# Loading wq straight into the tile that the matmuls read, in two halves and in its own column order

## The chip, the cores and the metric

The kernel runs on one core of a Trainium2 chip. The time is the device time of one execution in microseconds (us). Three runs of the kernel before gave 731.84, 732.01 and 732.11 us; the median, 732.01 us, is the number to compare with.

## The reference: what is computed

Two attention blocks, A and B, with the same shapes and their own inputs; their outputs are put side by side (16 x 64 x 1280). One block:

```python
B, Sq, D, H, Sk, Dh = 16, 64, 640, 32, 512, 128
q = (x @ wq).reshape(B, Sq, H, Dh).transpose(0, 2, 1, 3)
scores = einsum("bhqd,bhkd->bhqk", q, k_cache) * Dh ** -0.5
p = softmax(scores)
o = einsum("bhqk,bhkd->bhqd", p, v_cache)
out = o.transpose(0, 2, 1, 3).reshape(B, Sq, H * Dh) @ wo
```

All inputs are bf16. k_cache and v_cache are 67.1 MB each per block, so 268.4 MB of the 295 MB that are moved; wq and wo are 5.2 MB each per block. Each byte of the caches is read once.

## The kernel before, in words

**Packs.** The work is cut into 128 packs. A pack is four heads of two batch entries: 1.05 MB of K, 1.05 MB of V. Four packs (`NJ = 4`, index j) share one pair of batch entries and so one transposed x. Eight such groups make a phase of 32 packs, in which the same 16 heads' columns of wq (2.6 MB) and rows of wo (2.6 MB) are used. There are four phases: two halves of the heads for each of the two blocks.

**Operations of pack n**, by the names in the plan: `LDK`, `LDV` (loads into rings of 6 and 4 packs), `KT` (VectorE transposes K in 32x32 blocks of 32-bit words, L702), `QP` (20 matmuls x times wq into PSUM, L688), `QE` (ScalarE copies q to SBUF, L694), `S` (scores, L712), `EX` (ScalarE exp with row sums, L741), `RC` and `NM` (reciprocal on VectorE, normalisation on GpSimd, L762), `TR` (p is transposed on TensorE, L774), `TE` (VectorE copies it to SBUF, L854), `PV` (L867), `OE` (L875), `OP` (times wo, L887), and after each fourth pack `OS` and, in the phases that finish a block, the store `ST`. Once per group x is loaded and transposed: `LDX`, `XT` (L662), `XE`, `XS` and `XC` (GpSimd copies it to `xT_ring`, L677).

**Order.** No order is found at run time. `build_plan` gives every operation a due time in packs (`n + AT[...]`), sorts each engine's operations by it, and derives semaphore waits from the tiles that they read and write; a wait that follows from another one is left out. Each engine then works through its list in order. All loads but the first x are issued by SyncE (SP), in one list sorted by a priority that is also counted in packs: `LDK(n)` has n - 4.6, `LDV(n)` n - 2.1, `LDWO` of phase 0 n - 1.9 and of later phases n - 1.4. SP issues a load only when its buffer is free; what stands behind it waits too. `LDV(n)` waits for `TR(n-3)` in this way. Packs -1 and -2 are run on zeros, so that TensorE's list can be a loop of four packs from the first pack on.

**wq before.** `LDWQ` loads the 2.6 MB of a phase as five transfers (one for each 128 rows of D, 4096 bytes in a row) into a staging tile `ws_sb`, laid out like wq itself. In phase 0 all five stand at the head of SP's list, ahead of K. Those of phase 1 are issued at priority 1.85, those of phases 2 and 3 spread over the phase before. Eight operations `WP` per phase (GpSimd, L656, 128 x 1280 elements each, two for each j) copy the staging tile to `wqp_sb`; within each head they put the column 64 j' + 2 r + t at the place 4 r + 2 j' + t. `QP` reads its weights with a step of four elements, so that one weight load holds the columns whose partner words one 32-bit transpose of K brings to the same row. `KT` reads the K row of a token as 64 words in order (two blocks of 32) and writes runs of two words.

**Zeroing at the start.** On VectorE, in this order: `VZ` (two slots of the V ring, L594), `BZ` (four PSUM banks, L598), `WZ` (half of wo, L602). The zeroing of `pT_sb` for pack -2 (`TE(-2)`, L852) stands at its due time, -0.57 and -0.53, which is after `KT(0)` at -0.67. GpSimd zeroes `pn_ring` (`NM(-1)`, L760).

Of the kernel before, what the change touches and what calls it, by code (L numbers as in the profile page):

```python
# [20 lines left out]
class Cfg:  # L21
    NK = 6
# [18 lines left out]
              OPZ=(1.65, 1.7), OSH=(1.75, 1.8), STH=(1.85, 1.9), FL1=1.3, FLM=1.68, FLC=1.82, WP0=(-1.6, -1.59, -0.7, -0.69, 0.25, 0.26, 1.25, 1.26),  # L41
              WP1=(-3.5, -2.55, -2.45, -1.5, -0.5, 0.5, 0.6, 1.5))


class Op:
# [41 lines left out]
def build_plan(dims, cfg, general):  # L87
# [18 lines left out]
    def add_output(n):  # L106
        g, j = n // NJ, n % NJ
        final = n >= 0 and dims["FINAL"](g // NBP)
        apart = 0 <= n < cfg.KSPLIT or n >= N - cfg.NARROW
        for b in range(0 if apart else 1, 2):  # L110
            tv = n + AT["PV"]
            op = add("sp", "LDV", (n, b), tv - 0.3, [],
                     [("v" if n >= 0 else "absent", n % cfg.NV, i) for i in ((b,) if apart else (0, 1))])
            loads.append((n - cfg.NV + AT["PV"] + 0.2 if n >= 0 else -99.0, 3, op))
        if n == N - 1:
            for a in range(2):
                add("pe", "TRH", a, n + AT["TRH"][a], [("pn", n % cfg.NPN, i) for i in (2 * a, 2 * a + 1)] + [("ident",)],
                    [("SB", 2), ("SB", 3)] if a == 0 else [("SB", 0), ("SB", 1)])
# [12 lines left out]
        if n > -2:  # L131
            add("pe", "TR", n, n + AT["TR"], [("pn", n % cfg.NPN, i) for i in range(4)] + [("ident",)],
                [("B", 4), ("B", 5)])
        for b in range(2):
            add("dve", "TE", (n, b), n + AT["TE"][b], [], [("B", 4 + b), ("pT", b, 0), ("pT", b, 1)])
        add("pe", "PV", n, n + AT["PV"], [("pT", b, a) for b in range(2) for a in range(2)] + [("v", n % cfg.NV, 0), ("v", n % cfg.NV, 1)],
            [("B", 4), ("B", 5), ("B", 6), ("B", 7)])
        add("act", "OE", (n, 0), n + AT["OE"][0], [], [("B", 4), ("B", 5), ("oT", 0)])
        if n == N - 2:
            add("act", "OEH", (n, 1), n + AT["OE"][1], [], [("B", 6), ("B", 7), ("oT", 1)])  # L140
            for s in range(2):
                add("pe", "OPH", (n, s), n + 1 + AT["OPY"][s], [("oT", 0), ("oT", 1), ("wo", j)], [("B", 6 + s)])
            return
        add("act", "OE", (n, 1), n + AT["OE"][1], [], [("B", 6), ("B", 7), ("oT", 1)])
        add("act", "ZO", n, n + AT["ZO"], [("zeros",)], [("B", 6), ("B", 7)])
        add("pe", "OP", n, n + AT["OP"], [("oT", 0), ("oT", 1), ("wo", j)], [("B", 6), ("B", 7)])
        if j == NJ - 1:
            bp = g % NBP
            add("dve", "OS", g, n + AT["OS"], [("acc", bp)], [("B", 6), ("B", 7)]
                + ([("out_sb", 0), ("out_sb", 1)] if final else [("acc", bp)]))  # L150
            if final:
                loads.append((n + AT["ST"], 5, add("sp", "ST", g, n + AT["ST"], [("out_sb", s) for s in range(2)], [("out_dram", g)])))
# [17 lines left out]
                add("act", "LDX", g, -21.0, [], [("xn", g % cfg.NXN)])  # L170
        add("pool", "XC", g, n0 + AT["XC"], [("xe", 0), ("xe", 1)] if first else [("xs", g % NBP)], [("xT", g % cfg.NX)])
    for ph in range(NPH):
        twp = [ph * PH + t for t in AT["WP1" if ph else "WP0"]]
        for kt in range(dims["KT"]):
            ready = (twp[-1] - PH if ph > 1 else AT["WP0"][-1]) + 0.5
            op = add("sp", "LDWQ", (ph, kt), twp[0] - 0.5 if ph else -20.0, [], [("ws", kt, j) for j in range(NJ)])
            loads.append((ready + 2.0 + 0.14 * PH * kt if ph > 1 else AT["PV"] + 0.15 if ph else -50.0, 1, op))
        for j in range(NJ):
            w = ph * NJ + j
            n0 = ph * PH + j  # L180
            for i in range(2):
                add("pool", "WP", (w, i), twp[2 * j + i], [("ws", kt, j) for kt in range(dims["KT"])], [("wqp", j, i)])
            if ph:
                loads.append((n0 - NJ + AT["LDWO"], 4, add("sp", "LDWO", w, n0 + AT["OP"] - 0.8 * NJ, [], [("wo", j)])))
            else:
                loads.append((n0 - 1.9, 4, add("sp", "LDWO", w, n0 + AT["OP"] - 0.8 * NJ, [], [("wo", j)])))
    if not general:
        add("pool", "PZ", 0, -9.95, [], [("zeros",)])
    add("dve", "VZ", 0, -9.9, [], [("v", i % cfg.NV, b) for i in (-2, -1) for b in range(2)])
    add("dve", "BZ", 0, -9.8, [], [("B", 4), ("B", 5), ("B", 6), ("B", 7)])  # L190
    add("dve", "WZ", 0, -9.7, [], [("wo", NJ - 2), ("wo", NJ - 1)])
    add("pool", "NM", -1, -1 + AT["NM"][3], [], [("pn", -1 % cfg.NPN, i) for i in range(4)])
    for n in range(-2, N):
        add_output(n)
        if n < 0:
            continue
        g, j = n // NJ, n % NJ
        add("pe", "QP", n, n + AT["QP"], [("xT", g % cfg.NX), ("wqp", j, 0), ("wqp", j, 1)], [("SB", 1)])
# [54 lines left out]
    for op in ops:  # L253
# [27 lines left out]
    def stand_in(d, op):  # L281
# [223 lines left out]
def mha_kernel(nc, blocks, out, cfg=None):  # L505
# [26 lines left out]
    with contextlib.ExitStack() as es:  # L532
# [2 lines left out]
        def sb(name, shape, dt):  # L535
            return es.enter_context(nc.sbuf_tensor(name, shape, dt))

        wqp_sb = sb("wqp_sb", [128, NJ, KT, 512], BF16)
        wo_sb = sb("wo_sb", [128, HPH, D], BF16)
        ws_sb = sb("ws_sb", [128, KT, NJ, 512], BF16)  # L540
# [70 lines left out]
        def em_LDWQ(e, op):  # L611
            ph, i = op.idx
            c = ph % NSUB * HPH * DH
            src = blocks[ph // NSUB][3].rearrange("(kt p) n -> p kt n", p=128)
            ins = e.dma_start(ws_sb[:, i].rearrange("p j c -> p (j c)"), src[:, i, c:c + NJ * 512])  # L615
            return ins, ins

        def em_LDWO(e, op):
# [33 lines left out]
        def em_WP(e, op):  # L652
            j, jj = op.idx[0] % NJ, op.idx[1]
            src = ws_sb[:, :, j].rearrange("p k (i j r) -> p k i j r", i=4, j=2)
            dst = wqp_sb[:, j].rearrange("p k (i r j two) -> p k i j r two", i=4, j=2, two=2)
            ins = e.tensor_copy(dst[:, :, :, jj], src[:, :, :, jj].rearrange("p k i (r two) -> p k i r two", two=2))  # L656
            return ins, ins

        def em_XT(e, op):
            first = last = None  # L660
            for kt in range(KT):
# [18 lines left out]
        def em_QP(e, op):  # L680
# [1 line left out]
            j = n % NJ  # L682
            xs = (n // NJ) % NX
            first = last = None
            w = wqp_sb[:, j].rearrange("p k (c f) -> p k f c", f=4)
            for f in range(4):
                for kt in range(KT):
                    last = e.matmul(ps[:, 1, f * 128:(f + 1) * 128], w[:, kt, f, :], xT_ring[:, xs, kt, :],  # L688
# [9 lines left out]
        def em_KT(e, op):  # L698
            n = op.idx
            dst = kt_ring[:, n % NKT].rearrange("p t j b k two -> p (t j) b (k two)").bitcast(F32)  # L700
            src = kn_ring[:, n % NK].rearrange("p a c -> p (a c)").bitcast(F32).rearrange("p (c h b l) -> p c h b l", h=8, b=2, l=2)
            ins = e.transpose(dst.rearrange("p c b (h l) -> p c h b l", h=8, l=2), src)  # L702
            return ins, ins

        def em_S(e, op):
# [224 lines left out]
        emitters = {k[3:]: f for k, f in locals().items() if k.startswith("em_")}  # L930

        ahead = {}

        def units(key):
            return 16 if key[0].startswith("d_") else 1

        def emit(e, op, p, taken):
            sem = sems[p]
            waits = [(s, v - taken.get(s, 0)) for s, v in op.waits]
            attach = None  # L940
            if waits and not op.dma and op.kind != "FL1":
                attach = waits.pop()
            for s, v in waits:
                e.wait_ge(sem[s], v * units(s))
            kind = "EXG" if p and op.kind == "EX" else op.kind
            first, last = emitters[kind](e, op)
            if last is None:
                e.sem_inc(sem[op.sem], units(op.sem))
                return
# [121 lines left out]
```

## Time and profile before

| | |
|---|---|
| median of three runs | 732.01 us |
| the profiled execution: time, span | 732.12 us, 730.4 us |
| TensorE (PE) busy, granted clock | 674.1 us, 92%; 0.99 |
| VectorE (DVE), ScalarE (ACT), GpSimd (POOL) busy | 514.5, 533.3, 417.9 us |
| bytes moved by DMA | 295.02 MB, mean 404 GB/s |

Rows of the timeline and of the chain give start and duration in us. Rows of a group give line, engine, operation, tiles and shape, the count, then total us and mean ns of one, then the idle time before them with what ended it. A row of stretches gives, for a stretch A:B, its length, the busy time of PE, PEld (weight loads), DVE, ACT and POOL with their instruction counts, the granted clock of TensorE, the busy share of the 16 DMA engines and the GB/s moved. Issue rows of the DMA view end with the KB of each transfer and the median us from issue to landing. "issue" in the chain or behind a row is time in which the engine waited for nothing that the profile shows.

### The profile page before, as it was taken

To read this page: it belongs to the slowest core of one execution; us is meant where nothing else is said; L and a number is where in the kernel's file an instruction comes from. 1 tells how busy PE (TensorE), PEld (TensorE's weight loads), DVE (VectorE), ACT (ScalarE), POOL (GpSimd) and SP (SyncE) were. 2 spreads that over 40 slices of the span, in tenths; PEclk is the share of its full clock that TensorE was granted. 3 is DMA by queue.
4 is the path that set the end of the run, shared out by engine and by line. 5 is a ranking of instruction groups with operands and counts; after the bars stand their busy time and mean duration, and the time that the engine had idled before them with its cause. 6 is when DMAs were issued, how large, how long until landed. Compare 5 with 4: busy or idle time off the path is not lost.

```text
span 730.4 us, 61195 instructions
## 1 busy us (share of the span) xinstructions
PE 674.1 (92%) x28502; PEld 530.3 (73%) x28502; DVE 514.5 (70%) x691; ACT 533.3 (73%) x1574; POOL 417.9 (57%) x596
## 2 busy tenths in 40 slices
PE   1679999999999999999997899999999799999998
PEld 1458778787777777777775677787777577787775
DVE  5447777777777766767765667677777567878775
ACT  1447878778787777777875677777778677878775
POOL 4436565666875455554884555465587446555552
PEclk9889999999999999999999999999999999999999
DMA  8999999999999999999999999999999999999993
GB/s 337 401 404 414 414 415 413 415 414 415 415 400 409 419 414 416 416 416 417 416 411 402 415 414 413 414 415 415 414 416 407 403 415 418 417 418 417 416 415 122
DMA packets 72336, 295.02 MB, mean 404 GB/s; under 512 B 7664, under 2 KB 20080, under 8 KB 55920
## 3 DMA queue, kind: packets, MB, share of 16 engines
q1 hardware_dynamic: 72160, 294.52, 100.0%
q8 instruction: 10, 0.16, 0.1%
q10 hardware_dynamic: 144, 0.16, 0.1%
q14 instruction: 22, 0.18, 0.1%
HBM read 292.03 MB, written 2.62 MB: 403 GB/s over the span
## 4 chain that ended last, share of the span: by engine, by line
PE 53%; DMA 32%; SPq 6%; DVE 3%; issue 3%; POOL 2%; ACT 1%; DVEq 0%; POOLq 0%
DMA xn_ring<-in_B_x_dram 14%; PE ps L867 12%; PE ps L887 11%; PE ps L688 11%; PE ps L712 10%; DMA kn_ring<-in_A_k_cache_dram 9%; PE ps L774 7%; DMA kn_ring<-in_B_k_cache_dram 5%; DMA wo_sb<-in_B_wo_dram 4%; SPq L631 4%; DVE kt_ring L702 2%; POOL pn_ring L762 2%; SPq L641 1%; DVE pT_sb L854 1%; SPq L615 1%
## 5 line engine op out<-in xcount | busy, mean ns | idle before, releaser
L762 POOL TENSOR_SCALAR pn_ring<-pn_ring,recip 128x512 bf16<-128x512 bf16 x508 | 343.4, 695 | 246.1 <-DVE recip L754 221.0
L702 DVE STREAM_TRANSPOSE kt_ring<-kn_ring 128x2048 f32<-128x2048 f32 x128 | 295.3, 2307 | 120.3 <-DMA kn_ring<-in_B_k_cache_dram 80.3
L741 ACT ACTIVATE pn_ring<-ps 128x512 bf16<-128x512 f32 x512 | 296.4, 592 | 5.7 <-PE ps L712 5.7
L854 DVE COPY pT_sb<-ps 128x1024 bf16<-128x1024 bf16 x256 | 168.4, 671 | 60.2 <-PE ps L774 60.2
L688 PE MATMUL ps<-xT_ring,wqp_sb 128*128 128x128 bf16 x2560 | 165.9, 220 | 11.6 <-POOL xT_ring L677 11.6
L867 PE MATMUL ps<-pT_sb,v_ring 32*128 32x64 bf16 x16448 | 162.2, 192 | 10.6 <-DVE pT_sb L854 4.6
L688 PEld LDWEIGHTS ps<-xT_ring,wqp_sb 128*128 128x128 bf16 x2560 | 157.5, 114 | 17.8 <-issue 11.8
L867 PEld LDWEIGHTS ps<-pT_sb,v_ring 32*128 32x128 bf16 x16448 | 147.0, 91 | 24.8 <-issue 12.5
L887 PE MATMUL ps<-wo_sb,oT_sb 128*128 128x320 bf16 x1024 | 163.5, 303 | 0.0
L875 ACT ACTIVATE oT_sb<-ps 128x256 bf16<-128x256 f32 x257 | 84.7, 381 | 95.1 <-PE ps L867 95.1
L712 PE MATMUL ps<-kt_ring,qs_ring 32*64 32x512 bf16 x4096 | 138.4, 380 | 4.8 <-issue 4.8
L694 ACT ACTIVATE qs_ring<-ps 128x512 bf16<-128x512 f32 x128 | 76.4, 597 | 76.5 <-PE ps L688 74.5
L774 PEld LDWEIGHTS ps<-ident,pn_ring 64*128 64x128 bf16 x4096 | 68.3, 95 | 77.0 <-ACT oT_sb L875 46.0
L887 PEld LDWEIGHTS ps<-wo_sb,oT_sb 128*128 128x128 bf16 x1024 | 90.4, 98 | 36.7
L741 ACT ACTIVATION_READ_ACCUMULATOR pn_ring<-ps 128x1 f32 x512 | 105.3, 206 | 0.0
L774 PE MATMUL ps<-ident,pn_ring 64*128 64x64 bf16 x4096 | 82.9, 191 | 22.8 <-POOL pn_ring L762 18.6
L712 PEld LDWEIGHTS ps<-kt_ring,qs_ring 32*64 32x64 bf16 x4096 | 53.4, 103 | 32.9 <-issue 5.5
L754 DVE RECIPROCAL recip<-rowsum 128x2 f32<-128x2 f32 x256 | 40.6, 158 | 27.6 <-ACT pn_ring L741 24.6
L879 ACT ACTIVATE ps<-zeros 128x256 f32<-128x256 bf16 x128 | 49.5, 387 | 4.1
L656 POOL COPY wqp_sb<-ws_sb 128x1280 bf16<-128x1280 bf16 x32 | 39.6, 1256 | 9.9 <-DMA ws_sb<-in_A_wq_dram 6.8
L668 ACT ACTIVATE xe_sb<-ps 128x640 bf16<-128x640 bf16 x32 | 22.9, 716 | 8.7 <-PE ps L662 8.6
L677 POOL COPY xT_ring<-xe_sb 128x640 bf16<-128x640 bf16 x16 | 11.5, 717 | 21.0 <-PE ps L774 21.0
(42 smaller groups left out, 103.5 us busy)
## 6 DMA issues: line engine op xcount, KB each, us to landing
kn_ring<-in_B_k_cache_dram SPq DMA_DIRECT2D x128, 512.0 KB, 16.1
v_ring<-in_B_v_cache_dram SPq DMA_DIRECT2D x62, 1024.0 KB, 16.5
kn_ring<-in_A_k_cache_dram SPq DMA_DIRECT2D x112, 512.0 KB, 11.4
v_ring<-in_A_v_cache_dram SPq DMA_DIRECT2D x56, 1024.0 KB, 14.8
kn_ring<-in_A_k_cache_dram SPq DMA_DIRECT2D x32, 256.0 KB, 8.6
v_ring<-in_A_v_cache_dram SPq DMA_DIRECT2D x16, 512.0 KB, 8.9
ws_sb<-in_A_wq_dram SPq DMA_DIRECT2D x10, 512.0 KB, 9.3
wo_sb<-in_A_wo_dram SPq DMA_DIRECT2D x8, 640.0 KB, 13.3
```

The source lines that it names most:

```text
L688: last = e.matmul(ps[:, 1, f * 128:(f + 1) * 128], w[:, kt, f, :], xT_ring[:, xs, kt, :], start=(kt == 0), stop=(kt == KT - 1))
L694: ins = e.activation(qs_ring[:, op.idx % NQ].rearrange("p f b q -> p (f b q)"), ps[:, 1, :], ACTF.Copy, scale=scale)
L702: ins = e.transpose(dst.rearrange("p c b (h l) -> p c h b l", h=8, l=2), src)
L712: last = e.matmul(ps[64 * b:64 * b + 64, i, :], qs_ring[rows, n % NQ, f, b, :], kt_ring[rows, n % NKT, :, f // 2, b, :, f % 2], start=(f = ...
L741: ins = e.activation(dst, src, ACTF.Exp, scale=1.0, accum_out=sum_of(h))
L762: ins = e.tensor_scalar(pn_view(h), pn_view(h), recip[:, h:h + 1], 1.0, ALU.mult, ALU.mult)
L774: last = e.transpose(pt_bank(b)[:, 64 * c:64 * c + 64], pn[rows, c, :], ident[rows, rows], tile_position=(64 * b, 0))
L854: ins = e.tensor_copy(pT_sb[:, b].rearrange("p t q -> p (t q)"), pt_bank(b))
L867: last = e.matmul(ps[:, 4 + i, 64 * b:64 * b + 64], v_ring[rows, n % NV, b, c, :], pT_sb[rows, b, c, :], start=(t == 0 and i < 2), stop=(t ...
L875: ins = e.activation(oT_sb[:, 2 * a:2 * a + 2, :], o_ps[:, 2 * a:2 * a + 2, :], ACTF.Copy)
L879: ins = e.activation(z_ps, zeros[:, :].unsqueeze(2).broadcast_to([128, 2, 128]), ACTF.Copy)
L887: last = e.matmul(out_ps[:, s, :], oT_sb[:, i, :], wo_sb[:, 4 * j + i, s * NH0:(s + 1) * NH0], start=(j == 0 and i == 0), stop=(j == NJ - ...
```

## The change

- The staging tile `ws_sb` and the copies `WP` are gone. `LDWQ` writes `wqp_sb`, which now has wq's own column order, in two transfers per phase: columns of j = 0, 1 and columns of j = 2, 3, each 1.31 MB in pieces of 2048 bytes.
- In phase 0 the first half stands ahead of K (priority -50), the second half behind K of pack 0 (-4.0 against -4.6). In later phases the halves have priority -4.4 and -2.4, counted from the phase's first pack, and wait until TensorE has done the last `QP` of the phase before that reads the columns. For this a mark `QS` lets the first matmul of the operation after every second `QP` raise a semaphore.
- Who waits for wq: for packs 0 and 1 TensorE itself, with a wait `GO` ahead of `QP(0)`; for the first half of later phases `XC` on GpSimd; for second halves `NM(., 3)` of the pack two before the first `QP` that needs it, also on GpSimd.
- `QP` reads its weights at the same step of four elements as before. The permutation goes into `KT`: it reads the K words with a step of two (first the even, then the odd words of a token) and writes as before.
- `WZ` goes from VectorE to GpSimd, behind `XC(0)`. `TE(-2)` goes ahead of `KT(0)`.

```diff
-              OPZ=..., WP0=(-1.6, -1.59, -0.7, -0.69, 0.25, 0.26, 1.25, 1.26),
-              WP1=(-3.5, -2.55, -2.45, -1.5, -0.5, 0.5, 0.6, 1.5))
+              WQ=(-3.2, -4.4))
...
-            add("dve", "TE", (n, b), n + AT["TE"][b], ...)
+            add("dve", "TE", (n, b), n + AT["TE"][b] if n > -2 else AT["KT"] - 0.01 + 0.002 * b, ...)
...
-            op = add("sp", "LDWQ", (ph, kt), twp[0] - 0.5 if ph else -20.0, [], [("ws", kt, j) for j in range(NJ)])
-            loads.append((ready + 2.0 + 0.14 * PH * kt if ph > 1 else AT["PV"] + 0.15 if ph else -50.0, 1, op))
+        for i in range(2):
+            op = add("sp", "LDWQ", (ph, i), ph * PH + 2 * i + AT["WQ"][0] if ph else -20.0, [],
+                     [("wqp", j) for j in (2 * i, 2 * i + 1)])
+            loads.append((ph * PH + 2 * i + AT["WQ"][1] if ph else (-50.0, -4.0)[i], 1, op))
...
-                add("pool", "WP", (w, i), twp[2 * j + i], [("ws", kt, j) for kt in range(dims["KT"])], [("wqp", j, i)])
+    add("pe", "GO", 0, AT["QP"] - 0.001)
-    add("dve", "WZ", 0, -9.7, [], [("wo", NJ - 2), ("wo", NJ - 1)])
+    add("pool", "WZ", 0, AT["XC"] + 0.001, [], [("wo", NJ - 2), ("wo", NJ - 1)])
...
+        if j % 2:
+            add("pe", "QS", n, n + AT["QP"] + 0.001)
...
-        if op.kind == "QP" and op.idx > 0:
-            op.deps = [d for d in op.deps if d.kind != "WP"]
+        if op.kind == "QP":
+            n, j = op.idx, op.idx % NJ
+            at[("GO", 0) if n < 2 else ("XC", n // NJ) if j < 2 else ("NM", 4 * (n - j) + 3)].deps += [d for d in op.deps if d.kind == "LDWQ"]
+            op.deps = [d for d in op.deps if d.kind != "LDWQ"]
...
+        if d.kind == "QP" and op.eng == "sp":
+            return at[("QS", d.idx | 1)]
...
-            ins = e.dma_start(ws_sb[:, i].rearrange("p j c -> p (j c)"), src[:, i, c:c + NJ * 512])
+            ins = e.dma_start(wqp_sb[:, :, 1024 * i:1024 * i + 1024], src[:, :, c + 1024 * i:c + 1024 * i + 1024])
...
-            src = kn_ring[:, n % NK].rearrange("p a c -> p (a c)").bitcast(F32).rearrange("p (c h b l) -> p c h b l", h=8, b=2, l=2)
-            ins = e.transpose(dst.rearrange("p c b (h l) -> p c h b l", h=8, l=2), src)
+            src = kn_ring[:, n % NK].rearrange("p a c -> p (a c)").bitcast(F32)
+            src = src.rearrange("p (t h b l j) -> p t j h b l", h=8, b=2, l=2, j=2)
+            ins = e.transpose(dst.rearrange("p (t j) b (h l) -> p t j h b l", j=2, h=8, l=2), src)
...
+            if op.kind == "QS":
+                marks.append(sem[op.sem])
+                return
...
+            if op.eng == "pe" and marks:
+                first.then_inc(marks.pop(), 1)
```

More of the change, by code (lines that the diff above doesn't have):

```diff
@@ L134, in add_output @@
         for b in range(2):
-            add("dve", "TE", (n, b), n + AT["TE"][b], [], [("B", 4 + b), ("pT", b, 0), ("pT", b, 1)])
+            add("dve", "TE", (n, b), n + AT["TE"][b] if n > -2 else AT["KT"] - 0.01 + 0.002 * b, [], [("B", 4 + b), ("pT", b, 0), ("pT", b, 1)])
         add("pe", "PV", n, n + AT["PV"], [("pT", b, a) for b in range(2) for a in range(2)] + [("v", n % cfg.NV, 0), ("v", n % cfg.NV, 1)],
@@ L180, in build_plan @@
             n0 = ph * PH + j
-            for i in range(2):
-                add("pool", "WP", (w, i), twp[2 * j + i], [("ws", kt, j) for kt in range(dims["KT"])], [("wqp", j, i)])
             if ph:
@@ L197, in build_plan @@
         g, j = n // NJ, n % NJ
-        add("pe", "QP", n, n + AT["QP"], [("xT", g % cfg.NX), ("wqp", j, 0), ("wqp", j, 1)], [("SB", 1)])
+        add("pe", "QP", n, n + AT["QP"], [("xT", g % cfg.NX), ("wqp", j)], [("SB", 1)])
+        if j % 2:
+            add("pe", "QS", n, n + AT["QP"] + 0.001)
         add("act", "QE", n, n + AT["QE"], [], [("SB", 1), ("qs", n % cfg.NQ)])
@@ L536, in sb @@
             return es.enter_context(nc.sbuf_tensor(name, shape, dt))
-        wqp_sb = sb("wqp_sb", [128, NJ, KT, 512], BF16)
+        wqp_sb = sb("wqp_sb", [128, KT, NJ * 512], BF16)
         wo_sb = sb("wo_sb", [128, HPH, D], BF16)
-        ws_sb = sb("ws_sb", [128, KT, NJ, 512], BF16)
         kn_ring = sb("kn_ring", [128, NK, 2, 2048], BF16)
@@ L650, in em_LDV @@
             return ins, ins
[L652 to L657, printed above, removed]
         def em_XT(e, op):
@@ L684, in em_QP @@
             first = last = None
-            w = wqp_sb[:, j].rearrange("p k (c f) -> p k f c", f=4)
+            w = wqp_sb[:, :, 512 * j:512 * j + 512].rearrange("p k (c f) -> p k f c", f=4)
             for f in range(4):
@@ L932, in mha_kernel @@
         ahead = {}
+        marks = []
         def units(key):
@@ L940, in emit @@
             attach = None
-            if waits and not op.dma and op.kind != "FL1":
+            if waits and not op.dma and op.kind not in ("FL1", "GO"):
                 attach = waits.pop()
@@ L944, in emit @@
                 e.wait_ge(sem[s], v * units(s))
+            if op.kind == "GO":
+                return
+            if op.kind == "QS":
+                marks.append(sem[op.sem])
+                return
             kind = "EXG" if p and op.kind == "EX" else op.kind
             first, last = emitters[kind](e, op)
+            if op.eng == "pe" and marks:
+                assert first is not last
+                first.then_inc(marks.pop(), 1)
             if last is None:
```

5 lines of the change are left out of this document (1 added, 4 removed).

## The prediction

> **What bounds the kernel now.** I read the page first, then the chain of waits in order of time, then stretches of the span, and last the time that loads take to land.
>
> ```profile
> span 730.4 us, 61195 instructions
> PE 674.1 (92%) x28502; PEld 530.3 (73%) x28502; DVE 514.5 (70%) x691; ACT 533.3 (73%) x1574; POOL 417.9 (57%) x596
> DMA packets 72336, 295.02 MB, mean 404 GB/s; under 512 B 7664, under 2 KB 20080, under 8 KB 55920
> ```
> ```profile
> 58.86 1.19 PE ps L887 x8
> 79.26 1.19 PE ps L887 x8
> ...
> 586.28 18.53 DMA kn_ring<-in_B_k_cache_dram
> 604.83 2.31 DVE kt_ring L702
> ...
> 717.15 1.15 PE ps L867 x128
> ```
> ```profile
> 3.00:9.00 6.00, 0.69 (x5) 0.45 (x5) 5.05 (x3) 0.70 (x1) 0.72 (x1) 1.00 0.93 326
> 9.00:19.00 10.00, 2.92 (x69) 2.71 (x73) 5.15 (x5) 0.60 (x1) 6.78 (x6) 1.00 1.02 420
> 20.00:40.00 20.00, 13.51 (x474) 9.45 (x465) 8.48 (x12) 8.77 (x25) 10.24 (x13) 0.83 1.03 400
> 40.00:60.00 20.00, 15.60 (x515) 11.72 (x515) 8.60 (x14) 10.47 (x32) 6.24 (x10) 0.83 1.03 406
> 60.00:190.00 130.00, 130.00 (x5692) 103.19 (x5695) 101.99 (x135) 105.21 (x312) 81.50 (x119) 1.00 1.02 415
> 200.00:220.00 20.00, 19.64 (x788) 15.29 (x781) 14.84 (x22) 15.97 (x49) 15.02 (x20) 1.00 1.03 401
> 240.00:360.00 120.00, 114.78 (x4879) 90.73 (x4876) 85.07 (x117) 91.46 (x272) 66.68 (x97) 1.00 1.02 416
> 620.00:700.00 80.00, 80.00 (x3463) 62.93 (x3450) 62.44 (x81) 64.22 (x191) 44.19 (x66) 1.00 1.02 417
> ```
>
> The page puts TensorE ahead (92%). The stretches show a second bound that is as tight: from 9 us on the DMA engines are never under a share of 1.02, at 415 to 417 GB/s, whether TensorE is full (60 to 190, 620 to 700) or starved (240 to 360, 5.2 us idle). The two paces are nearly one number. Four packs on TensorE take 79.26 - 58.86 = 20.40 us, 5.10 us a pack. A pack's K and V are 2.097 MB and its quarter of an x load 0.04 MB; 2.138 MB in 5.10 us would be 419 GB/s, a little over the 415 that the DMA engines give. The landing times say how deep their queue is:
>
> ```profile
> kn_ring<-in_A_k_cache_dram SPq DMA_DIRECT2D x53, 512.0 KB, 9.9
> v_ring<-in_A_v_cache_dram SPq DMA_DIRECT2D x24, 1024.0 KB, 9.5
> ...
> v_ring<-in_A_v_cache_dram SPq DMA_DIRECT2D x4, 512.0 KB, 8.4
> ```
> ```profile
> v_ring<-in_A_v_cache_dram SPq DMA_DIRECT2D x22, 1024.0 KB, 17.4
> kn_ring<-in_A_k_cache_dram SPq DMA_DIRECT2D x40, 512.0 KB, 17.2
> ```
> ```profile
> xn_ring<-in_A_x_dram ACTq DMA_DIRECT2D x1, 160.0 KB, 2.3
> ```
>
> These are issues between 56 and 190 us, between 240 and 360 us, and the one load into an idle queue, 2.3 us. V waits behind others for 8.4 to 9.5 us in phase 0 (some 4 us more than its own 2.5 us of transfer and a 2.3 us landing need), and for 17.4 us later. So the queue is not empty after the start, TensorE never decides for longer than the DMA engines allow, and the end is set by bytes: 295.02 MB at 415 GB/s are 711 us, and around them lie the start, the slow stretches (326, 400, 401, 406 GB/s) and the last packs after the last landing. Only what changes the start, the rate of wq's own bytes, or lets the queue run dry can change the time.
>
> **The change part by part.** The sum is made against the profiled execution, 732.12 us around a span of 730.4; that is 0.11 us over the median of 732.01.
>
> ```profile
> 0.93 2.39 SPq L615 DMA_DIRECT2D ws_sb<-in_A_wq_dram  x5
> 7.90 2.19 DVE L602 MEMSET wo_sb<- 128x2560 uint32 x1 [0.52 <-issue]
> 12.22 2.45 POOL L656 COPY wqp_sb<-ws_sb 128x1280 bf16<-128x1280 bf16 x2 [6.80 <-DMA ws_sb<-in_A_wq_dram]
> 14.83 2.31 DVE L702 STREAM_TRANSPOSE kt_ring<-kn_ring 128x2048 f32<-128x2048 f32 x1 [4.74 <-DMA kn_ring<-in_A_k_cache_dram]
> 15.48 2.29 PE L688 MATMUL ps<-xT_ring,wqp_sb 128*128 128x128 bf16 x20 [11.58 <-POOL xT_ring L677]
> 17.20 1.03 DVE L852 MEMSET pT_sb<- 128x512 uint32 x2
> 17.68 1.80 POOL L760 MEMSET pn_ring<- 128x2048 bf16 x1
> 18.38 1.78 PE L867 MATMUL ps<-pT_sb,v_ring 32*128 32x64 bf16 x128 [0.60 <-DVE pT_sb L852]
> 20.08 1.07 PE L712 MATMUL ps<-kt_ring,qs_ring 32*64 32x512 bf16 x32
> ```
>
> *Start.* K of pack 0 has 1.31 MB of wq ahead of it, not 2.62. At 326 to 420 GB/s that is 3.1 to 4.0 us: KT(0) starts at about 11.2 and ends at 13.5. QP(0) waits only for its half of wq (1.47 MB with x, at 326 GB/s from 2.3 us: some 7 us) and for XC. TE(-2), 1.03 us, now lies in VectorE's wait for K, so PV(-2) is done before KT(0) ends. S(0) starts near 14 where it started at 20.08: TensorE is some 6 us early. GO stops everything behind it on TensorE, but S(0) would wait for KT(0) until 13.5 anyway. WZ on GpSimd costs 5120 elements at 1.80 us per 2048, 4.5 us; behind XC (about 6.2 us) it ends near 10.7, NM(-1) at 12.5, and TR(-1) needs that only after S(0), near 15. This 2.5 us is its cover; without it TR(-1) moves.
>
> For the end these 6 us count as nothing: they are no bytes. They are needed, though. Before, the 2.62 MB of phase 1's wq were issued at 40.63 us and filled the DMA queue for 6.3 us while TensorE was slow. They now go in about 28 packs later. The queue's excess of 4 us in phase 0 becomes 4 - 6.3 + 6, or 3.7 us: not dry. If TensorE gained under 2.3 us, the queue would run dry.
>
> *The start's rate.* Between 3 and 9 us 326 GB/s moved, 89 under 415, which is 1.3 us lost with wq alone at the head of the queue. Half of the wq there may halve it, or the loss may belong to the start whatever is loaded. Ends -1.3 and 0; I take half, -0.6.
>
> *Pieces of 2048 bytes for 4096.* No row has 2048. The pieces of V and K (4096, 8192 bytes) move at 415. The stretch 200 to 220 takes in most of phase 1's wo, pieces of 1280 bytes, and moves 401, some 0.7 us lost. Between these, by the inverse of the piece, 2048 lies about halfway: 0.35 us per phase, 1.4 for four. Ends 0 and 1.4; with neither row nearer I take 0.7.
>
> *Copies.* The 32 WP are 32 x 1.256 = 40 us of GpSimd, which is 57% busy. Two stand on the chain, near 197 and 549 us, 1.21 us each. Both lie where the DMA queue is full, so nothing is gained. XC and NM(., 3) now carry waits for wq; behind them stand NM, then TR. The first half goes into the queue just ahead of V of the pack two before the phase, the second just ahead of V of its first pack, and PV needs that V at about the time that QP or TR needs the half: PE would wait for V if it did not for wq. SP waits for QS about 0.4 packs (2 us) longer than for the TR in its place; the queue is 8 to 17 us deep. TensorE's wait at each boundary grows (wq and wo together are 5.2 MB, 12.6 us, in place of 6.3) and shrinks by as much in the phase before. Sum for this: 0. QS adds a semaphore, no instruction: 0.
>
> *KT.* Same 2048 words, read with a step of two words.
>
> ```profile
> L702 DVE STREAM_TRANSPOSE kt_ring<-kn_ring 128x2048 f32<-128x2048 f32 x128 | 295.3, 2307 | 120.3 <-DMA kn_ring<-in_B_k_cache_dram 80.3
> L656 POOL COPY wqp_sb<-ws_sb 128x1280 bf16<-128x1280 bf16 x32 | 39.6, 1256 | 9.9 <-DMA ws_sb<-in_A_wq_dram 6.8
> L677 POOL COPY xT_ring<-xe_sb 128x640 bf16<-128x640 bf16 x16 | 11.5, 717 | 21.0 <-PE ps L774 21.0
> L688 PEld LDWEIGHTS ps<-xT_ring,wqp_sb 128*128 128x128 bf16 x2560 | 157.5, 114 | 17.8 <-issue 11.8
> L887 PEld LDWEIGHTS ps<-wo_sb,oT_sb 128*128 128x128 bf16 x1024 | 90.4, 98 | 36.7
> ```
>
> No row has VectorE read like this. The nearest: WP writes single words 8 bytes apart, and its 640 elements more than the dense XC take 0.54 us, no more each than XC's; QP's weights, read 8 bytes apart, take 114 ns where dense ones take 98. So 0 to 16%, 0 to 0.37 us. VectorE is busy 102 us of 130, 4.0 us of a pack's 5.1, and takes either: 0. The far end is half rate, 2.3 us more per pack; that is the first rival.
>
> [...]
>
> Sum: 732.12 - 0.6 + 0.7 = 732.2; against the median, 732.1.
>
> **Rivals.** *First, slower: KT's read costs.* At half rate it is 4.6 us, VectorE 6.3 us a pack, and 128 x 6.3 + 14 (first S) + 10 (717.15 to the end, less a pack) = 830 us. It decides from about 1.1 us more per KT, where VectorE reaches 5.1; below 1.5 us more (295.02 MB / 128 / 415 = 5.55 us a pack on average) bytes still hide most of it. For it: nothing in the trace excludes it. Against: the WP and weight rows.
>
> *Second, slower: the queue runs dry near 50 us.* TensorE's first pass through its loop stops without a wait, at even distances:
>
> ```profile
> 25.89 1.10 PE L867 MATMUL ps<-pT_sb,v_ring 32*128 32x64 bf16 x115 [1.64 <-issue]
> 32.37 1.49 PE L712 MATMUL ps<-kt_ring,qs_ring 32*64 32x512 bf16 x19 [4.81 <-issue]
> 45.24 0.77 PE L774 MATMUL ps<-ident,pn_ring 64*128 64x64 bf16 x22 [3.98 <-issue]
> 51.63 0.57 PE L867 MATMUL ps<-pT_sb,v_ring 32*128 32x64 bf16 x51 [0.42 <-issue]
> ```
>
> 6.48, 12.87 and 6.39 us apart: instructions seem to come in every 6.4 us. If each batch is fetched when the one before is entered, all of it moves with the earlier start. If they come at a fixed time, TensorE gains nothing, and the queue lacks 2.3 us: 734.5 us.
>
> *Third, faster.* wq at the head was the cause of the slow start, and part of 20 to 60 us (400 and 406 GB/s, 1.2 us under 415) goes too, with pieces of 2048 for nothing: -1.3 - 1.2, 729.6 us.
>
> **How the numbers follow.** 0.2% of 732, 1.5 us, is about what a measurement of this kernel can tell from no change. No measurable change, 730.5 to 733.5 around 732.1: 0.45. Third rival, and a gain that I don't see: 0.25. First rival: 0.15, all of it far above. Second: 0.1. Both small prices at their full size together with a short dry spell: 0.05. Faster 0.25, same 0.45, slower 0.30. The likeliest case alone has 730.8 to 733.5. Leaving out the first rival, the range goes from 728.5 to 738.
>
> **What would show it.** KT's mean at 2.31 us or not, before all else. S(0) near 14 us. The stops of TensorE 6 us earlier, or where they were. The DMA share from 40 to 60 us at 1.0 and V landing in about 8 us: not dry. L656 gone, GpSimd near 380 us. Idle of TensorE gathered after 190, 380 and 560 us. The bytes unchanged and the packets some 2560 more. I am wrong if KT is over 3.4 us, if the DMA rate in 60 to 190 rises above 415 (then bytes were not the bound and the 6 us count), or if the last landing and the last PV move apart.

## The result, and the profile after

The changed kernel takes 734.73 us (median of six, 734.41 to 735.42), the kernel before 731.93 beside it. The ratio is 1.0039, with a 95% interval of 1.0026 to 1.0052: 2.8 us slower. The profiled execution took 734.41 us around a span of 732.7, 2.3 us over the one of before; it is the fastest of its six.

The page of the changed kernel, its first lines and the group of KT:

```profile
span 732.7 us, 61145 instructions
PE 679.0 (93%) x28502; PEld 533.0 (73%) x28502; DVE 513.8 (70%) x690; ACT 533.2 (73%) x1574; POOL 383.9 (52%) x565
...
DMA packets 74704, 295.02 MB, mean 403 GB/s; under 512 B 7472, under 2 KB 19888, under 8 KB 58288
...
L699 DVE STREAM_TRANSPOSE kt_ring<-kn_ring 128x2048 f32<-128x2048 f32 x128 | 295.4, 2308 | 116.1 <-DMA kn_ring<-in_B_k_cache_dram 77.4
```

The bytes are the same, in 2368 packets more. GpSimd is 34 us freer. KT reads with a step of two words at 2308 ns; it took 2307. So the first rival is out.

The timeline of the changed kernel's start, all engines; start and length in us, then the idle time in brackets:

```profile
8.19 2.29 PE L684 MATMUL ps<-xT_ring,wqp_sb 128*128 128x128 bf16 x20 [4.32 <-DMA wqp_sb<-in_A_wq_dram]
...
10.43 2.31 DVE L699 STREAM_TRANSPOSE kt_ring<-kn_ring 128x2048 f32<-128x2048 f32 x1 [1.85 <-DMA kn_ring<-in_A_k_cache_dram]
...
14.71 1.93 PE L709 MATMUL ps<-kt_ring,qs_ring 32*64 32x512 bf16 x32
```

TensorE's first pass through its loop, the stops that the second rival turned on:

```profile
27.19 1.39 PE L709 MATMUL ps<-kt_ring,qs_ring 32*64 32x512 bf16 x19 [4.51 <-issue]
...
39.67 0.77 PE L771 MATMUL ps<-ident,pn_ring 64*128 64x64 bf16 x22 [4.19 <-issue]
...
46.34 0.57 PE L864 MATMUL ps<-pT_sb,v_ring 32*128 32x64 bf16 x51 [0.91 <-issue]
```

S(0) starts at 14.71 us where it started at 20.08, and the stops come 5.2, 5.6 and 5.3 us earlier. All that the change does at the start is there, and yet the end is later. Stretches of the span say where it went. The columns are the stretch, its length, busy time of TensorE, its weight loads, VectorE, ScalarE and GpSimd, then TensorE's clock, the DMA share and GB/s. First the changed kernel:

```profile
0.00:40.00 40.00, 20.24 (x654) 14.72 (x656) 18.81 (x17) 14.81 (x39) 14.29 (x20) 0.93 0.97 373
40.00:60.00 20.00, 19.09 (x693) 14.76 (x688) 12.59 (x18) 11.46 (x35) 8.82 (x13) 0.89 1.03 409
60.00:100.00 40.00, 40.00 (x1763) 31.62 (x1761) 30.98 (x41) 32.15 (x95) 24.37 (x36) 1.00 1.02 410
180.00:184.00 4.00, 4.00 (x123) 3.05 (x107) 3.19 (x7) 3.86 (x13) 1.07 (x2) 1.00 0.90 311
180.00:200.00 20.00, 20.00 (x885) 15.81 (x866) 15.47 (x22) 16.32 (x49) 11.07 (x17) 1.00 1.00 392
360.00:420.00 60.00, 48.64 (x1980) 37.80 (x1978) 34.20 (x46) 36.50 (x108) 27.51 (x41) 0.94 1.03 407
540.00:600.00 60.00, 49.46 (x2009) 38.49 (x2006) 35.18 (x48) 38.04 (x114) 26.50 (x39) 0.97 1.03 407
```

The kernel before, without the row for 40 to 60 us (406 GB/s), which the prediction shows:

```profile
0.00:40.00 40.00, 18.12 (x606) 13.61 (x614) 20.96 (x18) 11.36 (x28) 19.47 (x27) 0.91 0.96 372
...
60.00:100.00 40.00, 40.00 (x1766) 31.65 (x1765) 31.17 (x41) 32.34 (x97) 24.37 (x36) 1.00 1.02 414
180.00:200.00 20.00, 20.00 (x885) 15.85 (x861) 15.52 (x22) 16.29 (x49) 16.22 (x21) 1.00 1.02 415
360.00:420.00 60.00, 52.06 (x2221) 40.98 (x2223) 38.49 (x52) 41.14 (x122) 37.64 (x52) 1.00 1.03 410
540.00:600.00 60.00, 53.63 (x2351) 42.26 (x2356) 39.73 (x55) 41.96 (x125) 37.13 (x52) 1.00 1.03 410
```

Rate times length gives the bytes; the stretches left out differ by at most 0.05 MB. The changed kernel moves 0.04 and 0.06 MB more up to 60 us, and then 0.16, 0.46, 0.18 and 0.18 MB less: 0.88 MB behind, which is 2.1 us at 415 GB/s. The profiled executions differ by 2.3 us. The chain of waits that ended last says why bytes count. In the changed kernel its last wait for a DMA is this load of K, which lands at 596.95 us; behind the transpose of that K the chain is TensorE's own work almost alone, to the end:

```profile
581.32 15.63 DMA kn_ring<-in_B_k_cache_dram
596.97 2.31 DVE kt_ring L699
```

The same pack's transpose started at 594.81 us before, 2.2 us earlier (the chain of before waits last for the K of two packs later, the row of 586.28 us that the prediction shows). So the account in bytes holds, and the question is why these stretches moved fewer. Three things are suspected: the pieces of 2048 bytes; a DMA queue that runs low, since SyncE is held or since wq no longer fills it at 40 us; and a wq that lands late at the boundaries.

On the second, SyncE's timeline in the changed kernel, ahead of phase 1:

```profile
171.66 1.18 SPq L634 DMA_DIRECT2D kn_ring<-in_A_k_cache_dram  x2
178.71 0.37 SPq L618 DMA_DIRECT2D wqp_sb<-in_A_wq_dram  x1
179.12 0.53 SPq L644 DMA_DIRECT2D v_ring<-in_A_v_cache_dram  x1
```

For 5.9 us (172.84 to 178.71) SyncE issues nothing: it waits for the mark QS, and V and K stand behind it. In the kernel before it waits 3.4 us at this place (172.83 to 176.27), for the buffer of V. From 180 to 184 us the queue gives 311 GB/s. Its depth shows in the landing times of loads issued between 56 and 190 us, 7.5 us for V where it was 9.5:

```profile
v_ring<-in_A_v_cache_dram SPq DMA_DIRECT2D x25, 1024.0 KB, 7.5
```

### The profile page after: what moved, and what is told of

Its sections match the earlier page's. It is cut to its first block, busy times and chain, and to the rows that moved or that the text cites. A ratio compares the mean times of both kernels' runs of the same rounds, so it can differ in the third digit from the quotient of the medians.

```text
span 732.7 us, 61145 instructions
## 1 busy us (share of the span) xinstructions
PE 679.0 (93%) x28502; PEld 533.0 (73%) x28502; DVE 513.8 (70%) x690; ACT 533.2 (73%) x1574; POOL 383.9 (52%) x565
## 4 chain that ended last, share of the span: by engine, by line
PE 71%; DMA 17%; SPq 6%; DVE 2%; issue 2%; ACT 1%; POOL 0%; POOLq 0%; DVEq 0%
PE ps L864 17%; PE ps L884 16%; PE ps L684 15%; PE ps L709 13%; PE ps L771 8%; DMA kn_ring<-in_B_k_cache_dram 5%; DMA xn_ring<-in_B_x_dram 4%; DMA kn_ring<-in_A_k_cache_dram 4%; SPq L634 3%; DMA wo_sb<-in_A_wo_dram 2%; DMA wo_sb<-in_B_wo_dram 2%; SPq L644 2%; DVE kt_ring L699 1%; PE ps L658 1%; DVE pT_sb L851 1%
## 5 line engine op out<-in xcount | busy, mean ns | idle before, releaser
L699 DVE STREAM_TRANSPOSE kt_ring<-kn_ring 128x2048 f32<-128x2048 f32 x128 | 295.4, 2308 | 116.1 <-DMA kn_ring<-in_B_k_cache_dram 77.4
L673 POOL COPY xT_ring<-xs_sb 128x640 bf16<-128x640 bf16 x16 | 11.5, 717 | 21.5 <-PE ps L771 19.1
```

What stands on the lines that cost most here:

```text
L699: ins = e.transpose(dst.rearrange("p (t j) b (h l) -> p t j h b l", j=2, h=8, l=2), src)
```

## The experiments

### Pieces of 2048 bytes in the kernel before (e2_pieces)

```diff
-        ws_sb = sb("ws_sb", [128, KT, NJ, 512], BF16)
+        ws_sb = sb("ws_sb", [128, 2, KT, 1024], BF16)
...
-            ins = e.dma_start(ws_sb[:, i].rearrange("p j c -> p (j c)"), src[:, i, c:c + NJ * 512])
+            ins = e.dma_start(ws_sb[:, :, i], src[:, i, c:c + NJ * 512].rearrange("p (h n) -> p h n", h=2))
...
-            src = ws_sb[:, :, j].rearrange("p k (i j r) -> p k i j r", i=4, j=2)
+            src = ws_sb[:, j // 2, :, 512 * (j % 2):512 * (j % 2) + 512].rearrange("p k (i j r) -> p k i j r", i=4, j=2)
```

> The kernel before, with its five loads of wq per phase cut into pieces of 2048 bytes (the staging tile is laid out in two halves); all else, times of issue included, is as before. Theory B (pieces of 2048 for 4096 bytes cost what the row of wo suggests): up to 1.4 us slower, 732.6 to 733.4. Theory A (the queue running low costs it, pieces are free): within 0.2 us of before, 731.8 to 732.2.

Measured: 733.72 us beside 731.86, 1.0030 (1.0017 to 1.0042), with 74896 packets for 72336. The pieces alone cost 1.9 us (1.2 to 3.1 by the interval), two thirds of the loss. Its stretches, same columns:

```profile
0.00:40.00 40.00, 18.04 (x583) 13.31 (x583) 20.97 (x18) 11.43 (x28) 19.22 (x27) 0.91 0.97 367
40.00:60.00 20.00, 14.28 (x533) 10.57 (x522) 7.69 (x12) 9.58 (x30) 6.41 (x10) 0.91 1.04 398
60.00:200.00 140.00, 140.00 (x6023) 110.86 (x6025) 109.39 (x147) 113.52 (x339) 88.10 (x127) 1.00 1.02 415
```

The rate falls where wq is loaded: phase 0's at the start (367 for 372, 0.20 MB) and phase 1's at 40 us (398 for 406, 0.16 MB). From 60 to 200 us no wq is loaded and it is 415. That makes 0.4 to 0.5 us a phase.

### Pieces of 1024 bytes (e7_quarter)

```diff
-        ws_sb = sb("ws_sb", [128, KT, NJ, 512], BF16)
+        ws_sb = sb("ws_sb", [128, NJ, KT, 512], BF16)
...
-            ins = e.dma_start(ws_sb[:, i].rearrange("p j c -> p (j c)"), src[:, i, c:c + NJ * 512])
+            ins = e.dma_start(ws_sb[:, :, i], src[:, i, c:c + NJ * 512].rearrange("p (h n) -> p h n", h=NJ))
...
```

> The kernel before with wq in pieces of 1024 bytes (2048 gave 733.72). If the price goes by the number of pieces, as theory B has it, the step from 4096 to 2048 bytes adds 2560 pieces and cost 1.9 us; 1024 adds 5120 more: 3 times 1.4 to 1.9 us in all, 736 to 737.6. If the 1.9 us came from something else in that layout: under 735.

Measured: 735.61 us beside 732.10, 1.0049 (1.0035 to 1.0063): 3.5 us, with 80016 packets. The other layout of the staging tile does not slow the copies, which take 1258 ns each (1255 in e2_pieces, 1256 before). The size of the pieces is the cause, but by the medians the price is less than in proportion to their number: 2560 more cost 1.9 us, 7680 more 3.5.

### The start's order alone, the staging kept (e6_start)

```diff
-            add("dve", "TE", (n, b), n + AT["TE"][b], [], [("B", 4 + b), ("pT", b, 0), ("pT", b, 1)])
+            add("dve", "TE", (n, b), n + AT["TE"][b] if n > -2 else AT["KT"] - 0.01 + 0.002 * b, [], [("B", 4 + b), ("pT", b, 0), ("pT", b, 1)])
...
+        for i in range(2 if ph == 0 else 0):
+            op = add("sp", "LDWQ", (ph, i), -20.0, [], [("ws", kt, j) for j in (2 * i, 2 * i + 1) for kt in range(dims["KT"])])
+            loads.append(((-50.0, -4.0)[i], 1, op))
...
```

> The kernel before with the changed order of the start alone: in phase 0 wq comes in two halves by columns (2048-byte pieces), the first ahead of K, the second behind K of pack 0, and TE(-2) ahead of KT(0); staging tile, copies WP and the early load of phase 1's wq stay. Theory bytes (the DMA queue sets the end, TensorE's earlier start is no bytes): 731.6 to 732.6, although S(0) starts about 5 us earlier. Rival (the 5 us count, and the change lost them again at the phases' ends): 727 to 730.

Measured: 732.45 us beside 732.10, 1.0001 (0.9992 to 1.0010). S(0) started at 15.76 us and the stops followed (27.41, 40.15 and 46.81 us). Its stretches:

```profile
40.00:60.00 20.00, 19.02 (x690) 14.72 (x690) 12.15 (x17) 11.01 (x33) 8.82 (x13) 0.87 1.03 407
60.00:100.00 40.00, 40.00 (x1766) 31.69 (x1765) 31.07 (x42) 32.25 (x97) 24.37 (x36) 1.00 1.02 414
```

A start that is 4.3 us earlier for TensorE buys nothing that can be measured where the queue is full; the rates are those of before. (Phase 0's wq has pieces of 2048 bytes here too; by e2 that hides a gain of up to 0.5 us.)

### wq of the later phases late, without the early start (e9_burst)

```diff
-            loads.append((ready + 2.0 + 0.14 * PH * kt if ph > 1 else AT["PV"] + 0.15 if ph else -50.0, 1, op))
+            loads.append((ph * PH - 8.0 if ph else -50.0, 1, op))
```

> The kernel before (staging tile, copies, pieces of 4096 bytes) with the five loads of wq of phases 1 to 3 in one go 8 packs ahead of the phase, so that wq and wo, 5.2 MB, come within some 10 packs of each phase's start as in the changed kernel, but early enough that nothing waits for wq. Theory bytes (it does not matter when the same bytes are moved, while the DMA queue is never empty): 731.8 to 732.4. If it is the crowding at the phases' starts that costs the rest of the changed kernel's loss (TensorE waits there in one piece, and its clock falls): 0.8 to 1.2 us slower, 732.7 to 733.2. If TensorE runs dry of filler near 45 us without being earlier (phase 1's wq is gone from there, TensorE is not 5 us ahead): the rate between 45 and 60 us falls under 390 and the time rises by 2 us or more, as the second rival of the prediction has it.

Measured: 737.84 us beside 732.09, 1.0076 (1.0063 to 1.0090): 5.75 us slower. Its stretches:

```profile
46.00:48.00 2.00, 2.00 (x14) 1.46 (x12) 2.00 (x3) 0.00 (x0) 1.93 (x3) 0.50 0.91 306
52.00:54.00 2.00, 2.00 (x48) 1.66 (x49) 1.33 (x3) 2.00 (x8) 1.10 (x2) 1.00 0.41 57
54.00:56.00 2.00, 2.00 (x144) 1.87 (x141) 1.60 (x3) 1.08 (x3) 2.00 (x4) 1.00 0.79 324
60.00:100.00 40.00, 40.00 (x1759) 31.57 (x1759) 31.39 (x41) 32.58 (x97) 23.48 (x36) 1.00 1.02 403
```

Without wq at 40 us the queue runs dry (57 GB/s between 52 and 54 us). Over the first 60 us it moves 363 GB/s where it was 383, 1.2 MB or 2.9 us; from 60 to 100 us another 0.44 MB, 1.1 us. The other 1.8 us are not missing bytes: from 100 to 600 us it moves as much as the kernel before to within 0.1 MB. Yet the K load that its chain waits for last lands at 610.75 us where it was 604.81; why was not taken apart.

### The same with pieces of 2048 bytes (e10_burst2k)

The edits of e9_burst and of e2_pieces together:

```diff
-            loads.append((ready + 2.0 + 0.14 * PH * kt if ph > 1 else AT["PV"] + 0.15 if ph else -50.0, 1, op))
+            loads.append((ph * PH - 8.0 if ph else -50.0, 1, op))
...
-            ins = e.dma_start(ws_sb[:, i].rearrange("p j c -> p (j c)"), src[:, i, c:c + NJ * 512])
+            ins = e.dma_start(ws_sb[:, :, i], src[:, i, c:c + NJ * 512].rearrange("p (h n) -> p h n", h=2))
...
```

> The same with pieces of 2048 bytes: both suspected costs of the changed kernel in the kernel before, without its later waits for wq. If costs add up, 1.6 to 1.9 us above the run with 4096-byte pieces. If pieces and place together make the whole loss, it lies within 0.4 us of the changed kernel's own time in the same call.

Measured: 740.00 us, 1.0102 (1.0087 to 1.0118), 2.2 us over e9_burst on the same chip. So the pieces add to whatever else is lost. The changed kernel, run once more beside it (below), is 5.0 us faster although its pieces are the same and its wq comes late too. Most of this lies in the first 100 us, where it moves 392 GB/s and e10_burst2k 373: 1.9 MB or 4.6 us. The queue of e10_burst2k runs dry there (110 GB/s from 46 to 48 us, 86 from 54 to 56). Up to 100 us the two differ in the order of the start and in the copies that belong to it. So the early start, worth nothing in e6_start, is worth up to 5 us once the filler (phase 1's wq at 40 us) is gone.

### The changed kernel again (e11_again)

No edit.

> The changed kernel once more, on the same chip as the two runs above: 734.4 to 735.0 by every theory; it is here to be compared with them.

Measured: 735.03 us, 1.0039 (1.0025 to 1.0052). The profiled execution took 735.42 us, 1.0 us over the first profile:

```profile
40.00:60.00 20.00, 19.12 (x688) 14.77 (x688) 11.85 (x16) 10.72 (x33) 8.79 (x13) 0.85 1.02 400
60.00:100.00 40.00, 40.00 (x1764) 31.71 (x1764) 31.20 (x42) 32.12 (x96) 24.29 (x36) 1.00 1.02 407
```

These are 0.18 and 0.12 MB less than in the first profile, 0.7 of the 1.0 us. After the start the queue is on the edge, and how often it is short differs from one execution to the next. Against e6_start, which has the early start and the filler (407 and 414), the two profiles of the changed kernel lie at 409 and 410, and 400 and 407: 0.12 to 0.42 MB, 0.3 to 1.0 us for the filler. The three runs below that have the same start and no filler lie between: 400 and 410 (e1_order), 400 and 408 (e3_nomark), 403 and 410 (e8_phase1).

### wq of the later phases behind V of its pack (e1_order)

```diff
-              WQ=(-3.2, -4.4))
+              WQ=(-3.2, -3.05))
```

> The changed kernel with one pair of numbers edited: in phases 1 to 3 the halves of wq stand right behind the V load whose buffer SyncE waits for anyway (priority -3.05 and -1.05 instead of -4.4 and -2.4), so that SyncE no longer holds V and K back while it waits for the mark QS. Theory A (SyncE's hold of 5.9 us before the first half at 178.7 us let the DMA queue run low, 303 and 319 GB/s from 180 to 184 us, and that is the largest single part of the 2.8 us): the dip goes, the wait of SyncE for QS falls from 22 us to near 0, and the time falls by 1.0 to 1.5 us to 733.2 to 733.8. Theory B (the 2048-byte pieces cost it): no change, 734.5 to 735. Theory C (wq that lands later stalls TensorE at the boundaries, and that counts): slower than 735.

Measured: 737.49 us beside 731.86, 1.0069 (1.0055 to 1.0083), 2.8 us over the changed kernel: the hold of SyncE is gone, and a worse wait stands in its place. The waits for block B's wq on GpSimd, total, count and largest in us (block A's adds 7.3 and 4.0 us in e1_order, and none in the changed kernel); e1_order:

```profile
POOL xT_ring L673 <- DMA wqp_sb<-in_B_wq_dram: 15.6, 2, 8.0
POOL pn_ring L759 <- DMA wqp_sb<-in_B_wq_dram: 11.6, 2, 6.4
```

The changed kernel:

```profile
POOL xT_ring L673 <- DMA wqp_sb<-in_B_wq_dram: 5.2, 2, 2.8
POOL pn_ring L759 <- DMA wqp_sb<-in_B_wq_dram: 3.4, 1, 3.4
```

GpSimd waits for wq, NM and with it TensorE stop behind it, and the stops reach TensorE's clock. TensorE's timeline and a stretch of e1_order:

```profile
554.49 2.30 PE L684 MATMUL ps<-xT_ring,wqp_sb 128*128 128x128 bf16 x20 [6.06 <-POOL xT_ring L673]
```
```profile
552.00:556.00 4.00, 1.51 (x15) 1.54 (x16) 0.00 (x0) 0.00 (x0) 2.37 (x4) 0.59 1.02 417
```

After a wait of 6.06 us the block QP takes 2.30 us for 1.28. The changed kernel has it twice, after its waits of 3.83 us near 379 and 3.40 us near 559, with the bytes still flowing:

```profile
380.00:384.00 4.00, 4.00 (x51) 2.99 (x47) 2.13 (x5) 0.30 (x1) 1.36 (x2) 0.50 1.03 391
561.00:563.00 2.00, 2.00 (x14) 1.51 (x13) 1.11 (x3) 0.13 (x1) 1.36 (x2) 0.50 1.06 396
```

After its waits of up to 2.14 us at the same boundaries the clock stays at 1.00 (386 to 420 and 566 to 600 us).

Bytes are not what e1_order lacks: by 600 us it is 0.80 MB behind the kernel before, 1.9 us, and it takes 5.6 us longer. Its chain last waits for a DMA here:

```profile
550.60 18.24 DMA wqp_sb<-in_B_wq_dram
```

From this landing of wq, at 568.84 us, the chain is TensorE's work almost alone, to the end, and nothing gives back what was lost before it.

### No mark, SyncE released by TR of the pack before (e3_nomark)

```diff
-              WQ=(-3.2, -4.4))
+              WQ=(-2.6, -3.15))
...
-        if j % 2:
-            add("pe", "QS", n, n + AT["QP"] + 0.001)
...
-            return at[("QS", d.idx | 1)]
+            return at[("TR", (d.idx | 1) - 1)]
```

> The changed kernel without the marks QS: SyncE waits for the TR that follows the QP in TensorE's list, and the halves stand just ahead of the V load that waits for the same TR (priority -3.15 and -1.15). If each mark delays the PV behind it (PV takes 1.17 us behind a mark and 1.15 without; four packs took 20.45 us in place of 20.40 between 60 and 190 us), four packs go back to 20.40 and the time falls by up to 1.6 us beyond what the order alone gives, where TensorE decides; if DMA bytes decide, it is the time of the run with the order alone, 733.2 to 733.8, within 0.3 us.

Measured: 734.96 us, 1.0036 (1.0023 to 1.0048): as the changed kernel. Its waits for wq are nearly those of e1_order (15.0 and 11.6 us), and it ends 2.5 us before it; the wq that its chain waits for last lands at 566.08 us, 2.8 us before that of e1_order. Two things move at once, so this shows only that neither the hold nor the marks are worth more than what a late wq costs.

### The hold taken away in phase 1 alone (e8_phase1)

```diff
-            loads.append((ph * PH + 2 * i + AT["WQ"][1] if ph else (-50.0, -4.0)[i], 1, op))
+            loads.append((ph * PH + 2 * i + AT["WQ"][1] + (0.35 if ph == 1 else 0.0) if ph else (-50.0, -4.0)[i], 1, op))
```

> The changed kernel, with the halves of wq moved behind the V load ahead of which they stand, in phase 1 alone, where loads land within 8 us and wq is early enough either way. Theory A (SyncE's hold there lets the queue run low): the rates of 303 and 319 GB/s from 180 to 184 us go back to 400 and more, and the time falls by 0.7 to 1.1 us, to 733.7 to 734.0. If the dip costs nothing: 734.6 to 734.9.

Measured: 734.61 us beside 732.10, 1.0033 (1.0021 to 1.0045). Its stretches:

```profile
180.00:184.00 4.00, 4.00 (x116) 3.01 (x104) 3.18 (x6) 3.71 (x12) 1.06 (x2) 1.00 1.00 398
180.00:200.00 20.00, 20.00 (x853) 15.68 (x841) 15.46 (x22) 16.43 (x49) 11.07 (x17) 1.00 1.03 405
```

The dip is gone (398 for 311 GB/s) and the boundary moves 0.26 MB more, which would be 0.6 us; but the median is 0.1 and 0.4 us under the two of the changed kernel, less than the runs can tell, and GpSimd now waits 2.5 us for phase 1's wq, which it did not. By its bytes, then, the hold is worth 0.6 us; the times neither show nor exclude it.

### The marks in the kernel before (e4_marks)

```diff
+        if j % 2:
+            add("pe", "QS", n, n + AT["QP"] + 0.001)
...
+            if op.kind == "QS":
+                marks.append(sem[op.sem])
+                return
...
+            if op.eng == "pe" and marks:
+                assert first is not last
+                first.then_inc(marks.pop(), 1)
```

> The kernel before, with the marks QS raised after every second QP and nobody waiting for them. If the marks cost about 25 ns each (64 of them, 1.6 us) and TensorE's pace counts in phase 0 and in the last 24 packs: 0.3 to 0.8 us slower, 732.2 to 732.8, and four packs take 20.45 us. If they are free: 731.9 to 732.1 and 20.40 us.

Measured: 732.19 us beside 731.86, 1.0005 (0.9996 to 1.0015), not told from nothing. In its chain a block PV takes 1.17 us in the packs with a mark and 1.15 in the others:

```profile
56.51 1.15 PE ps L869 x128
...
61.59 1.17 PE ps L869 x128
```

### K fetched two packs further ahead (e5_ring)

```diff
-    NK = 6
+    NK = 8
...
-    KLEAD = 2.5
+    KLEAD = 4.5
```

> The changed kernel with a K ring of 8 packs in place of 6 (in the space of the staging tile) and K loaded two packs further ahead. If what is left of the loss is the queue running low while SyncE or TensorE waits (at 60 us, at 182 us), it goes: 733.2 to 733.8, and K and V land later in phase 0 (over 11 us in place of 8). If the ring does not matter because bytes and pieces decide: 734.4 to 735. If more K ahead puts V and wq later and TensorE stalls at the phases' ends, as in the run with wq behind V: above 735.

Measured: 737.94 us beside 732.10, 1.0078 (1.0065 to 1.0092), 3.2 us over the changed kernel. The queue does stay fuller in phase 0 (413 GB/s from 60 to 100 us), but more K ahead puts V, wq and wo later at the boundaries, and TensorE falls behind there: the last DMA that its chain waits for is a load of wo, which lands at 583.28 us. By 600 us it is only 0.44 MB behind the kernel before, 1.1 us, and it takes 5.8 us longer. Its loads are done earlier, seen from the end, than in the kernel before, which moves 419 GB/s at this distance from its end (702 to 710 us):

```profile
708.00:716.00 8.00, 8.00 (x404) 6.14 (x389) 6.02 (x7) 6.30 (x19) 3.93 (x6) 1.00 0.90 350
```

## Why the prediction was right or wrong

The forecast was no measurable change, 732.1; the kernel became 2.8 us slower. The time lies in the range, on the side that had 0.30. Of the cases named, "both small prices at their full size together with a short dry spell" comes nearest to what happened, and it had 0.05. That the second rival's 734.5 us is near the time measured is luck: TensorE did gain its 5 us at the start, and most of the loss is the pieces.

**Right.** *What bounds the kernel*: bytes and queue, up to the last K that the chain waits for. The loss is 0.88 MB of missed transfers in the profiles, and the early start by itself changes nothing (e6_start). *KT at no cost*: 2308 ns with the step of two words, 2307 without. The prediction's far end, half rate, was the author's assumption, since no row of before had VectorE read with this step; the 4.6 us that it would have meant did not show. *The start*: S(0) at 14.71 where "near 14" stood, and the stops moved with it, so they do not come at fixed times; the prediction's guess that a batch of instructions is fetched when the one before is entered fits this, but no run shows the fetch. *The copies*: 34 us of GpSimd freed, no time gained. *The start's rate*, -0.6: in the first 40 us the changed kernel moved 373 GB/s with pieces of 2048 bytes and e2_pieces 367 with the same pieces, 0.24 MB or 0.6 us; e6_start, with the same order and pieces, moved 371, 0.4 us by the same count. These are single profiles.

**Wrong, the size of a term: "Pieces of 2048 bytes for 4096", taken at 0.7 between 0 and 1.4.** It measures 1.9 us (e2_pieces) and 2.2 (e10_burst2k against e9_burst), above the upper end by both medians. That smaller pieces move more slowly was right (398 GB/s for 406 from 40 to 60 us, e2_pieces). The 1.4 came from wo's 0.7 us a phase for pieces of 1280 bytes and an interpolation by the inverse of the piece, that is, by the number of pieces. The price of wo fits (pieces of 1024 bytes measure 3.5 us, 0.9 a phase); the interpolation does not, for the first 2560 pieces cost 1.9 us and the next 5120 only 1.6. The prediction then took half of the 1.4, with no row that spoke for less at 2048 bytes.

**Wrong, a step: "The queue's excess of 4 us in phase 0 becomes 4 - 6.3 + 6, or 3.7 us: not dry."** Removing the filler and starting early do cancel in the main: by 100 us e9_burst, which has neither filler nor early start, is 1.6 MB behind the kernel before, and the changed kernel 0.06 MB. But V lands in 7.5 us where it took 9.5, 2 us less depth and not 0.3, and between 40 and 100 us the changed kernel moves 0.12 to 0.42 MB less than e6_start, 0.3 to 1.0 us. The second rival's mechanism holds in part: not since TensorE gained nothing, as it had it, but, it seems, since 5.3 us of start against 6.3 us of filler leave the queue short at moments.

**Wrong, a step: "SP waits for QS about 0.4 packs (2 us) longer ...; the queue is 8 to 17 us deep."** The 2 us is near: 5.9 us where it was 3.4. The depth is what failed, for a landing time was taken for spare depth. Of the 7.5 us in which V lands in phase 0, the load needs by the prediction's own estimate 2.5 for its transfer (1.05 MB at 415 GB/s) and 2.3 for its landing (the x load into an idle queue), which leaves 2.7, and the queue ran low at 180 us. By its bytes this is up to 0.6 us (e8_phase1); the runs can't tell it from nothing.

**Right in this kernel, not in general: "Sum for this: 0" for the waits at the boundaries.** The changed kernel's boundaries at 380 and 560 us lose 0.18 MB each, 0.9 us together, which is the pieces' price of two phases (0.4 to 0.5 us each) and leaves nothing for the waits. In e1_order, with wq later by one load of V, the waits do cost. This also limits "Only what changes the start, the rate of wq's own bytes, or lets the queue run dry can change the time": e1_order and e5_ring miss bytes for 1.9 and 1.1 us and lose 5.6 and 5.8 us.

Together: -0.6 for the start, 1.9 for the pieces, 0.4 for the stretch from 60 to 100 us (0.16 MB) and 0.6 for the hold make 2.3 us, the difference of the profiled executions. With 0.3 to 1.0 for the filler and 0 to 0.6 for the hold it is 1.6 to 2.9 us, so the agreement to a tenth is luck. The pieces are shown by runs that change nothing else. The other terms are read from the bytes of profiles set side by side; no run isolates them in time, and how the 0.9 us between the loss and the pieces divides stays open.

## What to carry to other kernels

Where the DMA queue never empties, price a change in bytes and in pieces (here 1.9 us for 2560 pieces more), and a start that is earlier for the compute engine at nothing (4.3 us of it measured 1.0001 in e6_start), unless it replaces work that kept the queue full (up to 5 us between e10_burst2k and the changed kernel). A staging tile that looks like an idle copy also buys the right to load early, at a quiet time, in wide pieces; when it goes, all three go. Bytes may bound a kernel and a wait still cost (e1_order misses bytes for 1.9 us and loses 5.6): behind the last load that the chain waits for, the chain here is the compute engine's own work for 125 us and more, and what that engine has lost by then stays lost. A landing time under a full queue is not spare depth: take off what the transfer needs by itself before holding the queue's issuer (here 7.5 us of landing left 2.7 by the estimate above, and a hold of 5.9 us took the rate to 311 GB/s).

## What the runs showed of the hardware

For 10.5 MB of wq, pieces of 2048 bytes cost 1.9 us more than 4096 (1.2 to 3.1, e2_pieces), and pieces of 1024 bytes 3.5 us (2.6 to 4.6, e7_quarter), in a queue that was full (DMA shares of 1.04 and 1.05 from 40 to 60 us, where phase 1's wq is loaded). TensorE's stops in the first pass of its loop nearly keep their distances when the pass starts 5 us earlier: 12.48 and 6.67 us between those shown, where they were 12.87 and 6.39. VectorE's 32-bit transpose of 128x2048 takes as long with a step of two words in its source (2308 ns) as without (2307). At the boundaries of the changed kernel TensorE's granted clock is 0.50 after its waits of 3.40 and 3.83 us, and 1.00 after those of up to 2.14 us; in e1_order, in the 4 us around the end of a wait of 6.06 us, it is 0.59. In e4_marks PV takes 1.17 us where its first matmul raises a semaphore, and 1.15 where it does not.
